# Remainder products in runs of two steps on four PSUM banks, and column sums of two rows together, in the gradient kernel of a spectral and gated-linear block

## The chip, the cores and the metric

The kernel runs on one core of one Trainium2 chip. The metric is the device time of one execution in microseconds; before the change it was 1488.78 us, the median of three runs (1486.05 to 1489.39). The kernel consists of one launch that computes the forward result and all gradients.

The engines are named as the profile names them: PE is TensorE (the matrix unit), PEld its weight loads, DVE is VectorE, ACT is ScalarE, POOL is GpSimd, SP is SyncE. Matrix results land in PSUM, which has eight banks of 512 fp32 values on each of 128 partitions.

## The reference

The reference is a block of a network with its gradients. Input x is 2048 rows of 576. Six rows of modulation come from a condition vector c. Then:

```python
h = layernorm(x) * (1 + ca) + sa
x = x + ga * irfft2(rfft2(h) * (w_r + 1j * w_i))
h = layernorm(x) * (1 + cb) + sb
g, u = h @ w_gate, h @ w_up          # 576 -> 4608
x = x + gb * ((g * u) @ w_down)      # 4608 -> 576
```

It returns this x and the gradients, for a given output gradient, of x, w_r, w_i, w_gate, w_up, w_down, c and w_mod (the matrix that makes the modulation). All tensors are bf16.

Two parts matter here. The products g and u have 576 as their contracted length: four full pieces of 128 and one of 64 for each. And the gradients of two modulation rows are sums over all 2048 rows of the gradient of h, and of that gradient times the normalized x: sums down the columns, which the kernel makes on PE with a matrix of ones.

## The kernel before

**Stages.** The kernel first turns the output gradient, computes the layer norms and the forward Fourier products, and, mixed in between as filler work for PE, the product of the output gradient with w_down transposed (`ghh_couple`, L364 to L403), which it stores in HBM. Then comes the longest part, a loop over 18 blocks of 256 hidden columns (`for p in range(NP)`, 239 to 1178 us). Then follow the backward pass of the second layer norm, the Fourier products backwards, and the last stage (from about 1365 us), a loop over 16 rows of 128 tokens that makes the gradient of x (`for j in range(18)`, L1393 on, shifted so that the pieces of three rows are under way at once). Forward output rows (`y_piece`, L1094 to L1121, matmuls at L1106) are filler for PE in the last stages.

**One block of the loop.** `gu_block(p)` computes g and u for 256 hidden columns and all 2048 tokens: two halves `fb` of 128 columns by four slices `sb` of 512 tokens, eight steps. After it, in program order: loads of the weights of the next block, the weight gradients of block p-1 (`grads`, filler turned straight on here), and the product that gives the gradient of the second layer norm's output (`gh2_block`, L963 to L977).

**A step** has ten matmuls of 512 columns: four full ones for g, four full ones for u, and one remainder of 64 rows for each. The remainder of g lies in rows 64 to 127 of the array, that of u in rows 0 to 63 (L802 and L803), and the two run side by side, into two different banks. ACT then copies g and u out of PSUM (L816, L817), and DVE makes g*u, and the products of a stored row block `ghh` with u and with g (L818 to L820). The copies go to a ring `g_r` of six buffers; the products to `xT`, which the next parts read. After the last slice of a half, g*u is stored to HBM on SP's queue (L822).

**The order now.** `gu_four` takes four steps at once. Steps 0 and 1 do their full matmuls first, then the remainders of all four steps follow in one run, then steps 2 and 3 do their full matmuls. Each of the four steps has its own pair of PSUM banks, by a fixed table, so that all eight are in use:

```python
GU_BANKS = ((0, 1), (2, 3), (6, 7), (4, 5))
```

A block so has two runs of four remainder pairs. In block 0 the order of the steps is another: (0,0) (0,1) (0,2) (1,0) and then (1,1) (1,2) (0,3) (1,3), since the last quarter of `h2T` (the turned input) arrives late.

**The last stage.** For each row j, PE does the inverse transform's last parts (`stage_bi`, L579 to L583; `stage_ai`, L593), ACT copies the gradient out as `gh`, DVE multiplies it by the normalized row `n` into `q`, and both go on to the gradient of x (L1408 to L1422). One row later, `column_sums(gq.pop(j - 2), 6, j - 2, 64)` adds the two rows to running sums in banks 6 and 7: four matmuls of 64 columns of ones (L1041), two halves by two operands. The operands of three rows are kept: `gh_r` and `q_r` are rings of three buffers.

**What sets the order.** PE's instructions stand in the order in which they are written (`tc.manual_schedule(engines={PE})`). The queues of the other engines are put in order by the planner of the tile framework, which may issue a load before work that is written ahead of it. Waits are set from the reads and writes of each buffer. `Fill` is a list of closures with an estimated cost each; `fill.run(us)` issues as many as the given time holds.

Of the kernel before, what the change touches and what calls it, by code (L numbers as in the profile page):

```python
# [14 lines left out]
MUL = mybir.AluOpType.mult  # L15
# [7 lines left out]
D = 576  # L23
F = 4608
NP = 18
# [56 lines left out]
def build(ctx, tc, A_x, A_w_r, A_w_i, B_w_gate, B_w_up, B_w_down, c_in, w_mod, grad_out,  # L82
          out_0, out_1, out_2, out_3, out_4, out_5, out_6, out_7, out_8):
    nc = tc.nc
    pe, ve, ac, po, sp = nc.tensor, nc.vector, nc.scalar, nc.gpsimd, nc.sync
# [10 lines left out]
    hh_d = dram("hh_d", [8, 128, 2 * NP, 256])  # L96
# [9 lines left out]
    bank = psp.tile([128, 8, 512], FP32, name="bank")  # L106
# [29 lines left out]
    def span(base, n, size):  # L136
        return [base + i * size for i in range(n)]

    GO, H2P = 9984, 28416
    H2T, ACC = 48896, 69376  # L140
    ST = 106240
# [16 lines left out]
    h2T = V(H2T, [16, 5, 128])  # L158
    acc = V(ACC, [16, D], FP32)

    mm, tt, ts, act = pe.matmul, ve.tensor_tensor, ve.tensor_scalar, ac.activation
# [48 lines left out]
    with tc.manual_schedule(engines={PE}):  # L210
# [485 lines left out]
        g_r = Ring(span(ST + 21504, 6, 1024), [512])  # L696
# [35 lines left out]
        def load_ghh(i):  # L732
            t = ghh_r.next()
            ghh[i] = t
            po.dma_start(t[:], ghh_d[i // 2, :, i % 2, :])  # L735
# [50 lines left out]
        def sbk():  # L786
            sbank[0] += 1
            return sring[sbank[0] % len(sring)]

        GU_BANKS = ((0, 1), (2, 3), (6, 7), (4, 5))  # L790

        def gu_four(p, steps):

            w = wgu[p]

            def cols(k):
                fb, sb = steps[k]
                return slice(128 * fb, 128 * fb + 128), slice(4 * sb, 4 * sb + 4)

            def rem(k):  # L800
                (bg, bu), (fs, js) = GU_BANKS[k], cols(k)
                mm(bank[:, bg, :], w[64:128, 8, fs], h2T[64:128, js, 4, :], k > 1, k < 2)  # L802
                mm(bank[:, bu, :], w[0:64, 8, fs], h2T[0:64, js, 3, :], k > 1, k < 2)  # L803

            def full(k):
                (bg, bu), (fs, js) = GU_BANKS[k], cols(k)
                for m in range(4):
                    mm(bank[:, bg, :], w[:, m, fs], h2T[:, js, m, :], k < 2 and m == 0, k > 1 and m == 3)  # L808
                for n, m in enumerate((0, 1, 2, 4)):
                    mm(bank[:, bu, :], w[:, 4 + n, fs], h2T[:, js, m, :], k < 2 and n == 0, k > 1 and n == 3)  # L810

            def evac(k):
                (bg, bu), (fb, sb) = GU_BANKS[k], steps[k]
                i, cs = 2 * p + fb, slice(512 * sb, 512 * sb + 512)
                g, u = g_r.next(), g_r.next()
                ac.copy(g[:], bank[:, bg, :])  # L816
                ac.copy(u[:], bank[:, bu, :])  # L817
                tt(xT[:, 0, fb, cs], g[:], u[:], MUL)  # L818
                tt(xT[:, 1, fb, cs], ghh[i][:, cs], u[:], MUL)  # L819
                tt(xT[:, 2, fb, cs], ghh[i][:, cs], g[:], MUL)  # L820
                if sb == 3:
                    sp.dma_start(hh_d[:, :, i, :].rearrange("g f x -> f g x"), xT[:, 0, fb, :].rearrange("f (g x) -> f g x", g=8))  # L822
            for k, (fb, sb) in enumerate(steps):
                i = 2 * p + fb
                if i + 2 < 2 * NP and i + 2 not in ghh and i != 1:
                    load_ghh(i + 2)
            full(0)
            full(1)
            for k in range(4):
                rem(k)  # L830
                if k < 2:
                    evac(k)
            full(2)
            evac(2)
            full(3)
            evac(3)

        def gu_block(p):

            order = [(fb, sb) for fb in range(2) for sb in range(4)]  # L840
            if p == 0:
                order = [(fb, sb) for fb in range(2) for sb in range(3)] + [(0, 3), (1, 3)]
            for k in (0, 4):
                gu_four(p, order[k:k + 4])
            if p == 0:
                load_ghh(3)

        def transposes(k):
            for fb in range(2):
# [187 lines left out]
        def column_sums(srcs, b, j, w):  # L1037

            for h in range(2):
                for i, a in enumerate(srcs):  # L1040
                    mm(bank[w * i:w * i + w, b + h, 0:288], ones[:, 0:w], a[:, 288 * h:288 * h + 288], j == 0, j == 15, skip_group_check=True)  # L1041
# [184 lines left out]
        RA, RB = ST, ST + 84480  # L1226
# [138 lines left out]
        gl_r = Ring(span(RA + 3456, 3, 1152) + [ACC + 15616], [D])  # L1365
        e_r = Ring(span(RA + 6912, 2, 1152), [288], FP32)
        H_r = Ring(span(RA + 9216, 2, 1152), [D])
        gh_r = Ring(span(RA + 11520, 2, 1152) + [ACC + 12160], [D])
        tg_r = Ring(span(RA + 13824, 2, 1152) + [RB + 3 * U], [D])
        t2_r = Ring(span(RA + 16128, 2, 1152), [D])  # L1370
        q_r = Ring(span(ST + 93312, 2, 1152) + [ACC + 13312], [D])
        wmT = V(ACC, [9, D])
        R2 = V(ACC + 10368, [D])
        o8l = V(RB + 11520, [9, D])
# [20 lines left out]
        for j in range(18):  # L1395
            if j < 16:
                if j and j + 2 < 16:
                    load_xg(j + 2)
                Hs[j] = stage_bi(j, Gt, e_r, H_r)
            if j < 2:  # L1400
                store_rev(6 + j, gws[6 + j])
            if 1 <= j < 17:
                jj = j - 1
                stage_ai(Hs[jj])
                gh = gh_r.next()
                ac.copy(halves(gh), bank[:, 2:4, 0:288])
                n = xl[jj]
                act(n[:], n[:], ACT.Identity, bias=nmr1[:, jj:jj + 1], scale=rstd1[:, jj:jj + 1])  # L1408
                gn, t2, q, s = tg_r.next(), t2_r.next(), q_r.next(), s_r.next()
                gq[jj] = [gh, q]  # L1410
                opc = mod[:, SCA, :]
                tt(gn[:], gh[:], opc, MUL)
                tt(q[:], gh[:], n[:], MUL)
                tt(t2[:], q[:], opc, MUL)
                act(gn[:], gn[:], ACT.Copy, scale=rstd1[:, jj:jj + 1], accum_out=s[:, 0:1])
                act(t2[:], t2[:], ACT.Copy, scale=nrs1[:, jj:jj + 1], accum_out=s[:, 1:2])
                ts(s[:, 0:1], s[:, 0:1], -1.0 / D, None, MUL)
                act(t2[:], n[:], ACT.Identity, bias=s[:, 0:1], scale=s[:, 1:2])
                tt(gn[:], gn[:], t2[:], ADD)
                tt(gn[:], gn[:], gl[jj][:], ADD)  # L1420
                o1 = gn
                po.dma_start(o1_v[:, jj, :], o1[:])  # L1422
                fill.run(2.2)
            fill.run(2.2)
            if j > 1:
                column_sums(gq.pop(j - 2), 6, j - 2, 64)
            while mdone < min(18, 6 * j // 5):
                k, i = mdone // 3, mdone % 3
                mod_grad(*mgs[k], i)
                if i == 2 and k + 2 < 6:  # L1430
                    load_wm2(mgs[k + 2][0], mgs[k + 2][2])
                mdone += 1
            if 5 <= j < 14:
                i = j - 5
                sp.dma_start_transpose(out=wmT[:, i, :], in_=w_mod[:, 128 * i:128 * i + 128])
# [100 lines left out]
```

## Time and profile before

| | value |
|---|---|
| profiled execution | 1488.78 us |
| its span, first to last instruction | 1486.9 us |
| PE busy | 1450.2 us (98%), 11108 matmuls |
| DVE busy | 765.9 us (52%) |
| ACT busy | 541.4 us (36%) |
| POOL busy | 347.6 us (23%) |
| granted PE clock, mean | 0.996 |
| remainders of g (L802) | 144, 379 ns each |
| column sums (L1041) | 64, 298 ns each |

The profile is of one execution. Matmuls overlap in it: each row's duration reaches from its start to its modelled end, so that matmuls which start 216 ns apart show 380 ns each. What a matmul costs on PE is therefore read from the distance of the starts. In a list of instructions in order of time, the columns are the start in us, the duration in us, engine, line, operation, operands with their shape (rows times columns of the array, then partitions by elements), and in brackets the idle time ahead of it and what ended it. In a table of stretches, the columns after the stretch's length are the busy time of PE, PEld, DVE, ACT and POOL with their instruction counts, then the granted clock, the share of the transfer engines, and GB/s.

### The profile page before, as it was taken

To read this page: it belongs to the slowest core of one execution; us is meant where nothing else is said; L and a number is where in the kernel's file an instruction comes from. 1 tells how busy PE (TensorE), PEld (TensorE's weight loads), DVE (VectorE), ACT (ScalarE), POOL (GpSimd) and SP (SyncE) were. 2 spreads that over 40 slices of the span, in tenths; PEclk is the share of its full clock that TensorE was granted. 3 is DMA by queue.
4 is the path that set the end of the run, shared out by engine and by line. 5 is a ranking of instruction groups with operands and counts; after the bars stand their busy time and mean duration, and the time that the engine had idled before them with its cause. 6 is when DMAs were issued, how large, how long until landed. Compare 5 with 4: busy or idle time off the path is not lost.

```text
span 1486.9 us, 28249 instructions
## 1 busy us (share of the span) xinstructions
PE 1450.2 (98%) x11108; PEld 973.0 (65%) x11108; DVE 765.9 (52%) x1651; ACT 541.4 (36%) x1048; POOL 347.6 (23%) x510
## 2 busy tenths in 40 slices
PE   8999999999999999999999999999999998999898
PEld 5444443677677677677677677677677666677666
DVE  6533596533533543543543543543543687678665
ACT  6756675212212212222222222222222366334566
POOL 1344322113213213213203203203202013232211
PEclk9999999999999999999999999999999999999999
DMA  9657986978568558559558558548558389667763
GB/s 346 180 148 161 228 238 163 213 144 186 126 117 188 127 113 191 123 115 193 126 110 188 118 122 196 123 110 196 126 102 182 78 238 293 218 210 199 241 222 101
DMA packets 417050, 252.79 MB, mean 170 GB/s; under 512 B 319730, under 2 KB 384692, under 8 KB 416660
## 3 DMA queue, kind: packets, MB, share of 16 engines
q1 hardware_dynamic: 388706, 166.53, 49.4%
q0 software_dynamic: 27440, 83.65, 18.3%
q8 instruction: 87, 1.43, 0.4%
q10 hardware_dynamic: 770, 0.80, 0.2%
q14 instruction: 47, 0.39, 0.1%
HBM read 98.52 MB, written 76.26 MB: 118 GB/s over the span
## 4 chain that ended last, share of the span: by engine, by line
PE 79%; DVE 6%; DMA 6%; ACT 4%; issue 3%; SPq 1%; POOL 1%; DVEq 0%; ACTq 0%; POOLq 0%
PE bank L808 9%; PE bank L857 8%; PE bank L810 8%; PE bank L904 8%; PE bank L908 8%; PE bank L963 5%; PE bank L1106 5%; PE bank L966 5%; PE bank L965 5%; PE bank L964 5%; PE bank L371 3%; PE bank L375 2%; PE bank L802 2%; DMA arena<-in_w_mod_dram 2%; PE bank L924 2%
## 5 line engine op out<-in xcount | busy, mean ns | idle before, releaser
L977 DVE TENSOR_TENSOR arena<-arena,bank 128x576 f32<-128x576 f32 x256 | 192.8, 753 | 305.1 <-PE bank L966 305.1
L816 ACT CAST arena<-bank 128x512 bf16<-128x512 f32 x144 | 86.5, 601 | 395.8 <-PE bank L803 387.5
L966 PE MATMUL bank<-arena 128*128 128x288 bf16 x576 | 164.5, 286 | 0.0
L963 PE MATMUL bank<-arena 128*128 128x288 bf16 x576 | 164.0, 285 | 0.4 <-DVE arena L975 0.2
L965 PE MATMUL bank<-arena 128*128 128x288 bf16 x576 | 164.3, 285 | 0.0
L964 PE MATMUL bank<-arena 128*128 128x288 bf16 x576 | 164.0, 285 | 0.0
L1106 PE MATMUL bank<-arena 128*128 128x288 bf16 x1152 | 151.5, 290 | 2.2 <-ACT arena L1109 2.2
L904 PE MATMUL bank<-arena 128*128 128x256 bf16 x1152 | 149.5, 273 | 1.9 <-DVE arena L890 1.8
L908 PE MATMUL bank<-arena 128*128 128x256 bf16 x1152 | 149.3, 273 | 0.0
L808 PE MATMUL bank<-arena 128*128 128x512 bf16 x576 | 148.2, 380 | 0.0
L810 PE MATMUL bank<-arena 128*128 128x512 bf16 x576 | 147.8, 379 | 0.0
L1106 PEld LDWEIGHTS <-arena 128*128 128x128 bf16 x1152 | 112.7, 99 | 35.4 <-issue 5.6
L857 PE MATMUL bank<-arena 128*128 128x288 bf16 x1024 | 128.1, 286 | 0.0
L820 DVE TENSOR_TENSOR arena<-arena 128x512 bf16<-128x512 bf16 x144 | 60.8, 422 | 123.3 <-ACT arena L816 116.1
L904 PEld LDWEIGHTS <-arena 128*128 128x128 bf16 x1152 | 110.8, 98 | 18.6 <-issue 5.2
L908 PEld LDWEIGHTS <-arena 128*128 128x128 bf16 x1152 | 112.3, 98 | 13.7
L857 PEld LDWEIGHTS <-arena 128*128 128x128 bf16 x1024 | 100.2, 98 | 28.2
L735 POOL DMA_DIRECT2D arena<-ghh_d x36 | 19.9, 553 | 393.2 <-DVE arena L819 385.8
L909 ACT CAST arena<-bank 128x256 bf16<-128x256 f32 x144 | 52.9, 373 | 144.6 <-PE bank L908 144.6
L810 PEld LDWEIGHTS <-arena 128*128 128x128 bf16 x576 | 56.4, 98 | 67.9
L808 PEld LDWEIGHTS <-arena 128*128 128x128 bf16 x576 | 53.4, 98 | 71.6 <-issue 15.3
L817 ACT CAST arena<-bank 128x512 bf16<-128x512 f32 x144 | 85.7, 595 | 12.1 <-PE bank L810 11.6
(269 smaller groups left out, 2304.8 us busy)
## 6 DMA issues: line engine op xcount, KB each, us to landing
ghh_d<-arena POOLq DMA_DIRECT2D x72, 256.0 KB, 3.9
arena<-ghh_d POOLq DMA_DIRECT2D x36, 512.0 KB, 5.8
hh_d<-arena SPq DMA_DIRECT2D x36, 512.0 KB, 4.1
arena<-hh_d SPq DMA_DIRECT2D x32, 576.0 KB, 7.1
out_dram<-arena POOLq DMA_DIRECT2D x67, 144.0 KB, 4.8
out_dram<-arena POOLq DMA_DIRECT2D x36, 256.0 KB, 5.1
arena<-in_B_w_down_dram POOLq DMA_DIRECT2D x18, 288.0 KB, 4.5
arena<-in_B_w_gate_dram POOLq DMA_DIRECT2D x18, 256.0 KB, 3.5
```

The source lines that it names most:

```text
L808: mm(bank[:, bg, :], w[:, m, fs], h2T[:, js, m, :], k < 2 and m == 0, k > 1 and m == 3)
L810: mm(bank[:, bu, :], w[:, 4 + n, fs], h2T[:, js, m, :], k < 2 and n == 0, k > 1 and n == 3)
L816: ac.copy(g[:], bank[:, bg, :])
L857: mm(bank[:, b0 + h, 0:288], sf[:, 0, fb, j, :], go[:, j, 288 * h:288 * h + 288], j == 0, j == 15)
L904: mm(bank[:, st["b"], 0:256], h2p[:, j, 128 * m:128 * m + 128], sf[:, 1 + w, :, j, :], j == 0, False)
L908: mm(bank[:, st["b"], 0:256], h2p[:, j, 128 * m:128 * m + 128], sf[:, 1 + w, :, j, :], False, j == 15)
L963: mm(o, xT[:, 1, 0, cs], wT[p][:, 0, 0, hs], True, False)
L964: mm(o, xT[:, 2, 0, cs], wT[p][:, 0, 1, hs], False, False)
L965: mm(o, xT[:, 1, 1, cs], wT[p][:, 1, 0, hs], False, False)
L966: mm(o, xT[:, 2, 1, cs], wT[p][:, 1, 1, hs], False, True)
L977: tt(dst, dst, src, ADD)
L1106: mm(bank[:, yb, 0:288], hl[:, fb % 18, 128 * (j % 2):128 * (j % 2) + 128], wdr[:, fb, 288 * h:288 * h + 288], fb == 0, fb == 35)
```

## The change

`gu_four` becomes `gu_step`, one step at a time. A step takes two banks from a ring of the four banks 0 to 3 (`sbk()`). Steps with an even `sb` do their full matmuls and then their remainder pair; steps with an odd `sb` do their remainder pair first and then the full ones. The remainders of an even step and of the odd step behind it so stand together. The load of `ghh` number 3 moves from behind block 0 to ahead of its last step.

In the last stage, the column sums are made on odd j only, for the two rows j-3 and j-2 together, and the rings of their operands get a fourth buffer each, in memory that is free there.

```diff
-        GU_BANKS = ((0, 1), (2, 3), (6, 7), (4, 5))
-
-        def gu_four(p, steps):
-
+        def gu_step(p, fb, sb):
+            i = 2 * p + fb
+            if i + 2 < 2 * NP and i + 2 not in ghh and (i != 1 or sb == 3):
+                load_ghh(i + 2)
+            js = slice(4 * sb, 4 * sb + 4)
+            cs = slice(512 * sb, 512 * sb + 512)
+            fs = slice(128 * fb, 128 * fb + 128)
+            bg, bu = sbk(), sbk()
             w = wgu[p]
...
-            full(0)
-            full(1)
-            for k in range(4):
-                rem(k)
-                if k < 2:
-                    evac(k)
-            full(2)
-            evac(2)
-            full(3)
-            evac(3)
+            odd = sb % 2
+
+            def rem():
+                mm(bank[:, bg, :], w[64:128, 8, fs], h2T[64:128, js, 4, :], odd == 1, odd == 0)
+                mm(bank[:, bu, :], w[0:64, 8, fs], h2T[0:64, js, 3, :], odd == 1, odd == 0)
+            if odd:
+                rem()
+            for m in range(4):
+                mm(bank[:, bg, :], w[:, m, fs], h2T[:, js, m, :], odd == 0 and m == 0, odd == 1 and m == 3)
+            for k, m in enumerate((0, 1, 2, 4)):
+                mm(bank[:, bu, :], w[:, 4 + k, fs], h2T[:, js, m, :], odd == 0 and k == 0, odd == 1 and k == 3)
+            if not odd:
+                rem()
+            g, u = g_r.next(), g_r.next()
+            ac.copy(g[:], bank[:, bg, :])
+            ac.copy(u[:], bank[:, bu, :])
+            tt(xT[:, 0, fb, cs], g[:], u[:], MUL)
+            tt(xT[:, 1, fb, cs], ghh[i][:, cs], u[:], MUL)
+            tt(xT[:, 2, fb, cs], ghh[i][:, cs], g[:], MUL)
+            if sb == 3:
+                sp.dma_start(hh_d[:, :, i, :].rearrange("g f x -> f g x"), xT[:, 0, fb, :].rearrange("f (g x) -> f g x", g=8))
 
         def gu_block(p):
 
             order = [(fb, sb) for fb in range(2) for sb in range(4)]
             if p == 0:
                 order = [(fb, sb) for fb in range(2) for sb in range(3)] + [(0, 3), (1, 3)]
-            for k in (0, 4):
-                gu_four(p, order[k:k + 4])
-            if p == 0:
-                load_ghh(3)
+            for fb, sb in order:
+                gu_step(p, fb, sb)
...
-        gh_r = Ring(span(RA + 11520, 2, 1152) + [ACC + 12160], [D])
+        gh_r = Ring(span(RA + 11520, 2, 1152) + [ACC + 12160, ACC + 16768], [D])
...
-        q_r = Ring(span(ST + 93312, 2, 1152) + [ACC + 13312], [D])
+        q_r = Ring(span(ST + 93312, 2, 1152) + [ACC + 13312, ACC + 17920], [D])
...
-            if j > 1:
-                column_sums(gq.pop(j - 2), 6, j - 2, 64)
+            if j > 1 and j % 2:
+                for i in (j - 3, j - 2):
+                    column_sums(gq.pop(i), 6, i, 64)
```

## The prediction

> **What bounds the kernel now.** I read the page first, then the busy time by stretches, then TensorE's timeline in three places (the gate and up products, an older stage that already has the order the change brings, the last stage), then ScalarE's timeline beside the first, and the waits of the last stage.
>
> The page says that TensorE works through the whole span at full clock:
>
> ```profile
> span 1486.9 us, 28249 instructions
> PE   8999999999999999999999999999999998999898
> PEclk9999999999999999999999999999999999999999
> ```
>
> The stretches say the same more exactly: from 465 to 1170 us, where the gate and up blocks lie, PE is busy for all 705 us; in the last stage (1350 on) it has holes.
>
> ```profile
> 465.00:1170.00 705.00, 705.00 (x5481) 502.22 (x5479) 300.01 (x554) 158.05 (x330) 145.24 (x204) 1.00 0.64 141
> 1350.00:1400.00 50.00, 47.82 (x386) 34.59 (x384) 37.09 (x87) 26.17 (x57) 11.48 (x21) 1.00 0.75 233
> 1400.00:1440.00 40.00, 37.27 (x284) 25.16 (x283) 26.99 (x79) 24.67 (x51) 9.94 (x17) 0.96 0.78 244
> ```
>
> "Busy" can hide short stops, so I checked one gate and up block by its starts. It runs from 438.76 (first full product) to 454.73 (first matmul of the next kind), 15.97 us. Its first half in TensorE's timeline (start, duration, line):
>
> ```profile
> 441.35 1.03 PE L810 MATMUL bank<-arena 128*128 128x512 bf16 x4
> 442.31 0.39 PE L802 MATMUL bank<-arena 64*128 64x512 bf16 x1
> 442.31 0.39 PE L803 MATMUL bank<-arena 64*128 64x512 bf16 x1
> ...
> 442.97 0.38 PE L802 MATMUL bank<-arena 64*128 64x512 bf16 x1
> 442.97 0.38 PE L803 MATMUL bank<-arena 64*128 64x512 bf16 x1
> 443.28 1.04 PE L808 MATMUL bank<-arena 128*128 128x512 bf16 x4
> ```
>
> Full matmuls start 0.216 us apart (28 of them from 443.28 to 449.33). The 64-row remainders go two at a time, a pair every 0.216 us. The run of them costs more at its two ends: four full ones from 441.35 are through at 442.21, the run starts at 442.31 (0.10 late); its four pairs need 0.864, but the next full matmul comes 0.97 after the first pair (0.11 late). So entering and leaving the remainders costs 0.20 us a run. The block adds up with nothing over: 64 x 0.216 + 8 pairs x 0.216 + 2 runs x 0.20 = 15.95 against 15.97. There is no stop in it that a different use of banks could take away. A whole iteration repeats every 55.6 us (the remainder runs at 442.31 and 1165.11 lie 13 iterations apart), without holes.
>
> The dO-times-Wd stage has the order that the change brings, runs of two pairs (its remainders are L378 and L379):
>
> ```profile
> 66.38 1.03 PE L375 MATMUL bank<-arena 128*128 128x512 bf16 x4
> 67.34 0.39 PE L378 MATMUL bank<-arena 64*128 64x512 bf16 x1
> 67.34 0.39 PE L379 MATMUL bank<-arena 64*128 64x512 bf16 x1
> 67.56 0.38 PE L378 MATMUL bank<-arena 64*128 64x512 bf16 x1
> 67.57 0.38 PE L379 MATMUL bank<-arena 64*128 64x512 bf16 x1
> 67.88 1.04 PE L371 MATMUL bank<-arena 128*128 128x512 bf16 x4
> ```
>
> 66.38 + 0.864 = 67.24, start at 67.34: 0.10. 67.34 to 67.88 is 0.54, less two pairs (0.432): 0.11. Again 0.20 a run, whatever its length.
>
> **The change: gate and up.** The number of matmuls, copies, products and transfers is the same; their order and banks change.
>
> Runs of remainders: before, two per block, 36 in 18 blocks. After, an even step ends with its pair and the odd step behind it begins with its own, so each couple of steps makes one run: four per block. In block 0 the order of steps is (0,0) (0,1) (0,2) (1,0) (1,1) (1,2) (0,3) (1,3), the second number giving the parity; that makes the runs [1,2] [3] [4,5] [6,7] [8], five. Blocks 1 to 17: 17 x 2 extra x 0.20 = +6.8 us. All on PE, which has no hole there to take it: on the path in full. Block 0: 3 extra, +0.6, less a shorter wait. There the pair of step (0,3) could have started at 251.02 (0.22 behind the pair at 250.80) but waited for a transfer of h2T until 251.73. In the new order that pair comes 6 x 8 x 0.216 + 6 x 0.216 + 3 x 0.20 + 0.10 = 12.37 us behind the block's start at 239.04, at 251.41, and waits 0.32 instead of 0.71: -0.4. Block 0: +0.2. Sum of the part: +7.0 us.
>
> Banks: all eight in fixed pairs become a ring of four (0 to 3), so a couple is written again two steps later. Does PE wait for ScalarE's copies? Their rows:
>
> ```profile
> 442.79 0.59 ACT L816 CAST arena<-bank 128x512 bf16<-128x512 f32 x1 [19.30 <-PE bank L803]
> 443.27 0.59 ACT L817 CAST arena<-bank 128x512 bf16<-128x512 f32 x1
> ```
>
> A copy starts 0.48 behind the start of the matmul it waits for (442.31), and two take 0.48 + 0.59 = 1.07. So a couple is free 1.55 us behind the start of its last pair. An even step's couple is written again after the odd step's pair and eight full matmuls, 0.216 + 0.216 + 0.11 + 1.73 = 2.27 us behind that start; an odd step's couple after the next even step's eight full ones and two pair places, about 2.2 us behind its last matmul. 0.6 us or more to spare: cost nothing, covered by 2.2 us of matmuls a step against 1.07 of ScalarE and three VectorE products of some 0.34 us spacing. If a copy came over 0.6 us late, that cover would be gone, at the excess per step.
>
> The Trainium skill, in "Perfetto Trace Analysis", section "Matmul Optimizations", wants all eight PSUM banks used, and so speaks against this part; by it the copies would come into view, at most 144 x 1.07 = 154 us, and the rows above say none of it. "TensorE: Matmul & The Clock Gate", section "Single matmul latency", gives a lone warm matmul about 166 ns over its streaming; were each end of a run to pay that, my estimate from that page for the 37 extra runs would be 12 us, and the measured 0.20 a run makes it 7.4.
>
> Loads: the loads of ghh stand at the same step boundaries as before; only number 3 moves by one step within block 0 (POOL's queue), and is needed in block 1, some 20 us later. The hh stores on SP and the weight loads on POOL wait for the same reads, within a few us, and are used at the next block, tens of us off. Cost nothing.
>
> **The change: column sums.** Today 16 runs of four 64-column matmuls, one a row; after, eight runs of eight. In the last stage:
>
> ```profile
> 1438.99 4.57 PE L1106 MATMUL bank<-arena 128*128 128x288 bf16 x36
> 1443.49 0.44 PE L1041 MATMUL bank<-arena 128*64 128x288 bf16 x4
> 1443.86 0.42 PE L579 MATMUL bank<-arena 128*128 128x288 bf16 x2
> ```
>
> The 36 matmuls start 0.1224 apart and are through at 1443.39; the run comes 0.10 later, and takes 0.37 where two pairs need 0.245: 0.22 us a run for entering and leaving. Eight fewer: -1.76 us of PE time. Not all is on the path: PE waits in this stage for others.
>
> ```profile
> PE bank L581 <- DVE arena L588: 2.6, 3, 1.7
> PE bank L1106 <- ACT arena L1109: 2.2, 3, 1.1
> ```
>
> Apart from one stop of 0.4 us at 1446.2 they lie before 1434, and a PE that is there 0.2 us sooner waits as much longer. The runs at 1437.54 and behind (the last eight rows, four runs saved) lie in a stretch that the chain of waits gives to PE almost throughout. So at least 4 x 0.22 = 0.9, at most 1.76; I take the middle, -1.3. The added buffer for gh and q only makes the wait for two rows possible: today a row's buffers are written again three rows later, after its sums, and no PE or ScalarE wait stands at them. The sums of row 14 move behind those of 15's place, ahead of the R2 copy; PE's work to the end is the same.
>
> **Sum.** +7.0 - 1.3 = +5.7 us on the profiled execution's 1488.78 (span 1486.9 and 1.9 around it), which is also the median of the three runs: 1494.5.
>
> **Rivals.**
> 1. The last stage gains nothing: the 0.2 us steps are all eaten by waits for VectorE. +7.0: 1495.8. The holes before 1434 speak for it, the PE chain behind against.
> 2. Other side, not slower: only PE's order is written by hand; the other queues are planned anew, and in the last stage VectorE's H product (L588) could come early enough that PE's waits for it and for the y copy go. They are worth 2.6 + 2.2 = 4.8 us: 1494.5 - 4.8 = 1489.7, no measurable change. It decides once more than some 3 us of these go. Against it: the L1109 waits hang on input transfers that the change leaves alone (the chain shows loads of A_x of 3 to 6 us there).
> 3. The same, to the bad: a queue order that adds a wait of the size of the largest now (1.7 us) once or twice in the last stage: +1.7 to +3.4, up to 1498.
> 4. Four banks are too few: copies come late by over 0.6 us in some steps. At 0.1 us a step 144 x 0.1 = 14 us: 1509. For it: in the older stage, where two couples turn, a remainder did wait 2.19 us for its copy (L383, at 235.46) while ScalarE had other rows. Against it: the slack worked out, and that ScalarE has nothing but these copies in a block.
> 5. The change does not do what it says: the extra ends are hidden and only the sums count: 1487.5. Against it stand the two 0.20s, on PE itself.
>
> **How the numbers follow.** Forecast 0.62, rival 1 0.16, rival 2 0.06, rival 3 0.10, rival 4 0.03, rival 5 0.03. A measurement tells about 0.2% (3 us) from no change: slower holds the forecast, 1, 3, 4: 0.91; same, 2 and a part of 5: 0.07; faster 0.02. Forecast and rival 1 span 1494.0 to 1495.8; the three runs before lie between 1486.05 and 1489.39, so a median may sit up to 2.7 lower by this alone, and rival 3 reaches 1498. Range 1491.0 to 1498.0; 2 and 4 and 5 are left out.
>
> **What would show it.** Right: runs of two remainder pairs every 4 us in the blocks, each 0.20 us over; a block of 16.36 us; an iteration of 56.0 instead of 55.6; the last stage's runs of eight matmuls 0.71 us long, and that stage about a microsecond shorter. Wrong: PE idle before the full products released by the ScalarE copies; an iteration still of 55.6; a last stage that moves by more than 2 us either way.

## The result and the profile after

| | before | after |
|---|---|---|
| median (range, number of runs) | 1488.26 us (1486.05 to 1489.39, 4) | 1498.84 us (1498.26 to 1499.59, 4) |
| profiled execution | 1488.78 us | 1498.26 us |
| its span | 1486.9 us | 1496.5 us |
| PE busy | 1450.2 us | 1457.6 us |

The change makes the kernel slower: after over before is 1.0073, with the interval 1.0056 to 1.0091. That is about 10.6 us, where 5.7 were forecast; 1498.84 lies outside the range of 1491 to 1498. The sign was right, the size was not.

The page of after, its span and the row of busy times:

```profile
span 1496.5 us, 28276 instructions
PE 1457.6 (97%) x11108; PEld 969.4 (65%) x11108; DVE 773.4 (52%) x1651; ACT 549.0 (37%) x1048; POOL 347.4 (23%) x510
```

The number of matmuls is the same, and PE's busy time is 7.4 us higher. To find where the span's 9.6 us arose I cut TensorE's timeline at four landmarks that both kernels have: the first full gate product, the first `gh2` product behind the last block, the first matmul of the last stage (L579), and the first matmul of the tail (before L1442, after L1424).

| us | before | after | difference |
|---|---|---|---|
| start to the first gate product | 239.04 | 238.88 | -0.16 |
| the loop over 18 blocks | 938.49 | 947.22 | +8.73 |
| between the loop and the last stage | 190.72 | 189.29 | -1.43 |
| the last stage | 109.13 | 111.49 | +2.36 |
| the tail | | | +0.1 |

The loop and the last stage are the two places that the change touches; both are worse than forecast (+7.0 and -1.3).

**The blocks look as forecast.** TensorE's timeline of after in one block (start, duration, line; L807 and L809 are the full products, L802 and L803 the remainders):

```profile
1170.57 1.03 PE L809 MATMUL bank<-arena 128*128 128x512 bf16 x4
1171.53 0.39 PE L802 MATMUL bank<-arena 64*128 64x512 bf16 x1
1171.54 0.39 PE L803 MATMUL bank<-arena 64*128 64x512 bf16 x1
1171.76 0.38 PE L802 MATMUL bank<-arena 64*128 64x512 bf16 x1
1171.76 0.38 PE L803 MATMUL bank<-arena 64*128 64x512 bf16 x1
1172.07 1.04 PE L807 MATMUL bank<-arena 128*128 128x512 bf16 x4
```

Runs of two pairs, as predicted, one every 4.1 us. Entering: 1170.57 + 4 x 0.216 = 1171.43, start at 1171.53, 0.10 late. Leaving: 0.54 from the first pair to the next full product, less two pairs of 0.216: 0.11. The block runs from 1169.71 to 1186.10, 16.39 us against 16.36 forecast and 15.97 before. No row of a block shows idle time released by the ScalarE copies.

The whole iteration, by the start of the Wd gradient in two blocks that follow each other, first in before (L857):

```profile
510.33 8.00 PE L857 MATMUL bank<-arena 128*128 128x288 bf16 x64
565.93 8.00 PE L857 MATMUL bank<-arena 128*128 128x288 bf16 x64
```

and in after:

```profile
513.72 8.00 PE L838 MATMUL bank<-arena 128*128 128x288 bf16 x64
569.75 8.00 PE L838 MATMUL bank<-arena 128*128 128x288 bf16 x64
```

56.03 us in after against 55.60 in before: +0.43 for two more runs, 0.215 a run.

**One wait stands in the loop in addition**, in block 1, where the period is 57.51 us instead of 56.03. TensorE's and ScalarE's timelines of after there (in brackets the idle time ahead and what ended it):

```profile
304.66 1.03 PE L885 MATMUL bank<-arena 128*128 128x256 bf16 x8 [1.32 <-ACT arena L911]
303.48 0.87 ACT L976 ACTIVATE arena<-arena 128x576 bf16<-128x576 bf16 x1 [14.54 <-DMA arena<-x_d]
304.25 0.35 ACT L911 CAST arena<-bank 128x256 bf16<-128x256 f32 x1
```

ScalarE stood 14.5 us before a transfer of x_d with the activation of `keep_n`, and the copy that PE needed stood behind it.

**The last stage is longer, not shorter.** PE's waits in it, after (waiting line and line waited for; us in total, number, longest):

```profile
PE bank L581 <- DVE arena L588: 3.5, 2, 2.4
PE bank L1087 <- ACT arena L1090: 3.2, 2, 2.5
PE bank L593 <- ACT arena L1387: 1.1, 1, 1.1
```

The first two are waits that before had too, larger now: 6.7 us against 4.8. The third, for the copy of `gh`, is new.

**Part of it is no property of the kernel.** After, TensorE's timeline behind the first of the waits for L1090:

```profile
1391.22 1.27 PE L1087 MATMUL bank<-arena 128*128 128x288 bf16 x9
1394.96 5.14 PE L1087 MATMUL bank<-arena 128*128 128x288 bf16 x27 [2.48 <-ACT arena L1090]
1400.03 0.68 PE L1022 MATMUL bank<-arena 128*64 128x288 bf16 x8
```

The 27 matmuls took 5.14 us, where 26 distances of 0.1224 and the last one's 0.29 make 3.47. The busy time by stretches of after shows why, ahead of the two waits of over 2 us and around them (the granted clock is the third number from the end):

```profile
1375.00:1393.00 18.00, 17.37 (x138) 12.56 (x137) 12.40 (x35) 7.02 (x14) 5.84 (x10) 1.00 0.65 202
1393.00:1402.00 9.00, 7.04 (x46) 4.52 (x46) 4.31 (x12) 7.47 (x18) 1.10 (x2) 0.81 0.79 253
1430.00:1442.00 12.00, 9.56 (x69) 6.03 (x67) 10.54 (x33) 8.55 (x19) 4.29 (x7) 0.86 0.60 167
```

The granted clock falls behind the wait. Such a slow spell costs 1.7 us each time (9.00 x (1 - 0.81), 12.00 x (1 - 0.86)). Before has one in its last stage, after two, and after run again (after_again, below) none. So a single profile's stage is compared both as it is and less its spells: before 109.1 and 107.4, after 111.5 and 108.1.

### The profile page after: what moved, and what is told of

Its sections match the earlier page's. It is cut to its first block, busy times and chain, and to the rows that moved or that the text cites. A ratio compares the mean times of both kernels' runs of the same rounds, so it can differ in the third digit from the quotient of the medians.

```text
span 1496.5 us, 28276 instructions
## 1 busy us (share of the span) xinstructions
PE 1457.6 (97%) x11108; PEld 969.4 (65%) x11108; DVE 773.4 (52%) x1651; ACT 549.0 (37%) x1048; POOL 347.4 (23%) x510
## 3 DMA queue, kind: packets, MB, share of 16 engines
q8 instruction: 87, 1.43, 0.4%
## 4 chain that ended last, share of the span: by engine, by line
PE 80%; DVE 8%; DMA 5%; ACT 4%; issue 2%; SPq 0%; POOL 0%; DVEq 0%; ACTq 0%; POOLq 0%
PE bank L807 9%; PE bank L809 8%; PE bank L838 8%; PE bank L885 8%; PE bank L889 8%; PE bank L944 5%; PE bank L947 4%; PE bank L945 4%; PE bank L946 4%; PE bank L1087 4%; PE bank L371 3%; PE bank L375 3%; PE bank L802 3%; DMA arena<-in_w_mod_dram 2%; PE bank L905 2%
## 5 line engine op out<-in xcount | busy, mean ns | idle before, releaser
L813 ACT CAST arena<-bank 128x512 bf16<-128x512 f32 x144 | 84.3, 585 | 384.8 <-PE bank L803 376.9
L807 PE MATMUL bank<-arena 128*128 128x512 bf16 x576 | 148.6, 380 | 0.0
L809 PE MATMUL bank<-arena 128*128 128x512 bf16 x576 | 147.8, 379 | 0.0
L807 PEld LDWEIGHTS <-arena 128*128 128x128 bf16 x576 | 50.4, 98 | 78.1 <-issue 30.6
L809 PEld LDWEIGHTS <-arena 128*128 128x128 bf16 x576 | 56.4, 98 | 67.9
L814 ACT CAST arena<-bank 128x512 bf16<-128x512 f32 x144 | 84.8, 589 | 22.5 <-PE bank L809 22.5
```

The costliest lines, as they stand in the source:

```text
L807: mm(bank[:, bg, :], w[:, m, fs], h2T[:, js, m, :], odd == 0 and m == 0, odd == 1 and m == 3)
L809: mm(bank[:, bu, :], w[:, 4 + k, fs], h2T[:, js, m, :], odd == 0 and k == 0, odd == 1 and k == 3)
```

## The experiments

Ratios are to the kernel before on the same chip, with a 95% interval. "Last stage" and "period" are measured as above.

### The two parts alone: g_only, g_only_c, g_only_d, s_only, s_only_c

g_only is before with the new `gu_step` alone, that is after with the last stage as before:

```diff
-        gh_r = Ring(span(RA + 11520, 2, 1152) + [ACC + 12160, ACC + 16768], [D])
+        gh_r = Ring(span(RA + 11520, 2, 1152) + [ACC + 12160], [D])
...
-        q_r = Ring(span(ST + 93312, 2, 1152) + [ACC + 13312, ACC + 17920], [D])
+        q_r = Ring(span(ST + 93312, 2, 1152) + [ACC + 13312], [D])
...
-            if j > 1 and j % 2:
-                for i in (j - 3, j - 2):
-                    column_sums(gq.pop(i), 6, i, 64)
+            if j > 1:
+                column_sums(gq.pop(j - 2), 6, j - 2, 64)
```

> The gate and up part of the change alone; the column sums stay one row at a time with three buffers. Theory 1 (the price is the ends of the remainder runs, 0.20 to 0.215 us each, and the last stage's loss belongs to the sums): blocks 2 to 16 repeat every 56.03 us instead of 55.60, the last stage from its first L579 to the first row sum of R2 keeps its 109.1 us, and the total is 7 to 9 us above the kernel before, the upper end if the 1.3 us wait of the first weight gradient products for a ScalarE copy in block 1 comes again. Theory 2 (the gate and up part shifts the last stage against its transfers): the last stage takes 111 us or more here, total 9 to 11 us above. Theory 3 (four banks too few): PE shows waits for the copies L813 or L814 in the blocks.

s_only is the opposite: these hunks alone, on before.

> The column sums of two rows together with the fourth buffer, on the kernel before; gate and up products as before. The prediction's working: 0.9 to 1.76 us faster, last stage 107.4 to 108.2 us against 109.1. Theory 1 (the pairing moves PE work behind waits, and the queues of ScalarE, VectorE and SyncE come out in another order): last stage 111 to 112 us, total 2 to 3 us slower, with a PE wait for the copy of the output row of over 2 us near the first sums. Theory 2 (the loss belongs to the shift by the gate and up part): last stage 108, total about 1 us faster.

The same two kernels again, beside after, on other chips:

> The gate and up part alone, again, on one chip with the change and the sums alone. Ratio 1.005 to 1.006 (7.5 to 9 us), with a loop of 946.2 us.

> The column sums alone, again. Leaving out 6.5 us of sums saved 2.1 us, a third; the pairing takes 1.76 us of PE time away, so by that price -0.6 us, ratio 0.9985 to 1.001. If the pairing's new queue order costs what the change shows over the gate and up part: ratio 1.0015 or more.

> The gate and up part alone, third time. The loop gives 7.7 us, 1.0052. Two runs gave 1.0051 and 1.0061, with chances of a further 1 us behind the loop. If that further 1 us is real, 1.0058 or more again; if not, 1.0055 or less.

| | median, us | ratio | period, us | last stage, us |
|---|---|---|---|---|
| g_only | 1497.14 | 1.0051 (1.0034 to 1.0069) | 56.03 | 110.01 |
| g_only_c | 1497.61 | 1.0061 (1.0045 to 1.0076) | 56.03 | 110.15 |
| g_only_d | 1497.78 | 1.0050 (1.0032 to 1.0068) | 56.03 | 109.05 |
| s_only | 1488.66 | 0.9999 (0.9986 to 1.0011) | 55.61 | 109.14 |
| s_only_c | 1491.66 | 1.0014 (1.0002 to 1.0026) | 55.60 | 109.54 |

The gate and up part costs some 8 us (the mean of the three ratios is 1.0054). Its loop is 945.96 to 946.86 us long against 938.49: +7.7, the median of the three being 946.16. The column sums, forecast at -1.3, change nothing in one measurement and cost 2 us in the other.

### The buffers alone don't matter: s_3buf

The paired sums with the two rings left at three buffers.

```diff
-            if j > 1:
-                column_sums(gq.pop(j - 2), 6, j - 2, 64)
+            if j > 1 and j % 2:
+                for i in (j - 3, j - 2):
+                    column_sums(gq.pop(i), 6, i, 64)
```

> The column sums of two rows together, with the rings of gh and q left at three buffers, on the kernel before. The queues stand in the same order as with four. If the fourth buffer is needed for the pairing to go without a wait: slower than the run with four buffers by 1 us or more, with ScalarE's copy of gh or VectorE's q waiting for PE's sums. If it is not: the same within 1 us.

1489.55 us, 1.0011 (0.9999 to 1.0024), last stage 108.82 us. The instructions of every engine stand in the same order as in s_only; the fourth buffers change no queue, and by this the time no more than can be measured.

### Four banks or eight: g_8banks

The order of after in the blocks, but with the fixed pairs of before, turned through all eight banks. To show it on top of after (the last stage as before):

```diff
+        gstep = [-1]
+
...
-            bg, bu = sbk(), sbk()
+            gstep[0] += 1
+            bg, bu = ((0, 1), (2, 3), (6, 7), (4, 5))[gstep[0] % 4]
```

> The gate and up part alone as in the first run, but each step takes the next of the four fixed pairs over all eight banks, as the kernel before has them. Order of the matmuls as after. Theory 1 (runs of remainders are the whole price): iteration 56.03 us, the same as with four banks. Theory 3 (four banks cost): 55.6 to 55.9 us.

1495.62 us in the profiled execution; loop 946.02 us. Its Wd gradients in TensorE's timeline:

```profile
512.36 8.00 PE L841 MATMUL bank<-arena 128*128 128x288 bf16 x64
568.39 8.00 PE L841 MATMUL bank<-arena 128*128 128x288 bf16 x64
```

The period is 56.03 us, the same to the hundredth as with four banks. The banks cost nothing, as forecast. The Trainium skill's wish for all eight banks ("Perfetto Trace Analysis", section "Matmul Optimizations") makes no difference here, 56.03 against 56.03.

### The price of a run: g_8runs

Every step ends with its own pair: eight runs a block instead of four (the last stage as before).

```diff
-            odd = sb % 2
+            odd = 0
```

> The gate and up part with every step ending in its own remainder pair, no step starting with it: eight runs a block in place of four (36 before, 73 in the change, 144 here). Theory 1 (0.20 to 0.215 us for each run): 71 runs more than the change's, blocks repeat every 56.03 + 4 x 0.21 = 56.9 us, 14 to 15.5 us slower than the gate and up part alone. Rival (a run costs less when it is short, as two pairs against four would hint): under 56.6 us.

1510.58 us. Its Wd gradients in TensorE's timeline:

```profile
518.76 8.01 PE L838 MATMUL bank<-arena 128*128 128x288 bf16 x64
575.65 8.01 PE L838 MATMUL bank<-arena 128*128 128x288 bf16 x64
```

The period is 56.89 us. With 36, 73 and 144 runs of remainders in the program the loop is 938.49, 946.15 and 961.84 us long. By period, two more runs a block cost 0.43, four more 0.86: 0.215 us a run both times (by the whole loop, block 0 included, 0.207 and 0.221). This line through three points is the explanation of the gate and up part; within some 0.01 us a run it leaves nothing for banks or copies. "TensorEngine Tiling (Array Packing)", section "Key Properties", in the Trainium skill says that a change of the tiling mode drains the TensorE, without a price; what these runs show is 0.215 us for going to 64-row tiles and back.

### The wait in block 1: after_again, after_k

after_again is the unchanged kernel after once more. after_k is after with `keep_n` of row 0 moved from block 1 to block 2:

```diff
-                    if i == 7:
-                        keep_n(p)
+                    if i == 7 and p > 1:
+                        keep_n(p if p > 2 else 1)
+                    if i == 15 and p == 2:
+                        keep_n(2)
```

> The changed kernel itself, timed again on one chip with the runs below. If its two parts simply add (gate and up alone measured 1.0051 of the kernel before, column sums alone 0.9999), the ratio is 1.005 to 1.006, 7 to 9 us, and the 1.3 us wait of block 1 and the 111.5 us of the last stage that its first profile shows were that execution's. If the parts act on one another, the ratio stays at 1.007 or more, and its profile shows a last stage over 111 us again.

> The changed kernel with the saving of normalized row 0 (load of x1, ScalarE's normalizing, store) moved from block 1 to block 2, so that in block 1 ScalarE has no load to wait for ahead of the copies of the weight gradients. If the wait of 1.3 us in block 1 stands in most executions: 1 to 1.5 us faster than the change. If it was that one execution's: the same within 0.7 us.

after_again: 1498.37 us, 1.0083 (1.0070 to 1.0096); its loop is 946.15 us, and the wait in block 1 isn't there. after_k: 1498.79 us, 1.0069 (1.0052 to 1.0087), the same as after beside it (below). So the 1.48 us of block 1 belong to that one profiled execution: of the ten profiles that have the new order in the blocks and `keep_n` in its old place, one has a wait of over 1 us there. It was a tempting cause and explains nothing of the median.

### Is PE's time in the last stage on the path: no_sums

Column sums of rows 0 and 15 alone, before's other lines.

```diff
-            if j > 1:
+            if j in (2, 17):
                 column_sums(gq.pop(j - 2), 6, j - 2, 64)
```

> The kernel before with the column sums left out for rows 1 to 14 (the sums are then over rows 0 and 15 alone); 56 matmuls and 14 runs of 64-column matmuls fewer, some 14 x 0.47 = 6.5 us of PE time. Prediction's step (PE bounds the second half of the last stage): at least 8 x 0.47 = 3.8 us faster, last stage 105 us or less against 109.1. Theory 1 (the last stage is set by the chain of transfers, ScalarE and VectorE, and PE's time there is spare): less than 1.5 us faster, last stage 108 us or more, PE's waits up from 5 to 10 us or more.

1485.04 us, 0.9986 (0.9975 to 0.9996). Fourteen runs of 0.37 + 0.10 us, 6.6 us of PE's time, are gone, and by the medians 2.1 us come out: a third. The last stage is 105.49 us, 3.6 shorter. PE's waits in it, no_sums:

```profile
PE bank L581 <- DVE arena L588: 5.1, 4, 1.8
PE bank L1106 <- ACT arena L1109: 2.0, 3, 1.0
PE bank L579 <- ACT arena L585: 0.4, 1, 0.4
```

Waits for the H product (L588) grow from 2.6 us in three places to 5.1 in four: what PE saves, it partly waits. This kernel's queues are planned anew too, so the third is no pure measure.

### More buffers: x5_row

If input transfers hold the last stage up, a fifth buffer for x should help.

```diff
-        x_r = Ring(span(RA, 3, 1152) + [ACC + 14464], [D])
+        x_r = Ring(span(RA, 3, 1152) + [ACC + 14464, ACC + 33600], [D])
```

> The kernel before with a fifth buffer for the rows of x in the last stage, so that a row's load waits less for the buffer to be given back. Theory 1 (the chain row of x loaded, ScalarE's normalizing, the copies queued behind it, is what PE waits for): ScalarE's waits for loads of A_x fall from 29.6 us, PE's waits in the last stage fall from 5.2 to under 2.5 us, 2 to 4 us faster. Rival (the order of VectorE and ScalarE's own work sets the pace): within 1 us of the kernel before.

1491.49 us, 1.0031 (1.0020 to 1.0042): slower, with a resource added and no work. ScalarE's waits for loads of x in the last stage did not shrink (21.1 us, before 21.2), PE's waits there grew from 4.8 to 7.0 us. The planner had put the queues of the other engines in another order. That this order is the cause is not shown, as no run has the fifth buffer in the old order; it turned the question from buffers to orders.

### The order of the other queues: pair_oldq, row_newq, after_oldq

PE's order in this program is written by hand; the tile framework plans the others. By the traces, the shortest edit from before's order to that of s_only moves 4 instructions on ACT, 39 on DVE, 4 transfers on SP and one on POOL, all in the last stage; the gate and up part alone moves one transfer, on POOL, in block 0. Two kernels separate the sums from the order. pair_oldq has the paired sums, but the last stage's instructions of the four engines are held in the order that before has, by ordering edges between neighbours that set no semaphore. row_newq has single-row sums (with the fourth buffers in place), and the engines are held in the order that was planned for the pairs. In the traces the last stage's instructions stand in the orders intended. The core of both (`_ORDER` lists the source lines of the last stage in the order wanted, engine by engine):

```diff
-        fill.flush()
+        fill.flush(); _enforce(tc, LOG)
...
+def _enforce(tc, log):
+    for e, want in _ORDER.items():
...
+        seq = [next(it[key]) for key in want]
+        for a, b in zip(seq, seq[1:]):
+            tc.add_manual_dep(b, a.name, mybir.DependencyInfo(mybir.DependencyClass.NoSync, mybir.DependencyReason.DATA), reason="order")
```

> The column sums of two rows together (four buffers) on the kernel before, but with the instructions of ScalarE, VectorE, GpSimd and SyncE in the last stage held in the order that the kernel before has. Only PE's order differs from before. If the planner's new queue order is what ate the pairing's gain: 0.6 to 1.8 us faster than the kernel before, ratio 0.9988 to 0.9996, and 1 to 3 us faster than the sums alone with their own queue order (0 to 2.3 us above before). If the moved PE work itself costs (less work ahead of a wait, more behind it): no faster than before, 0 to 2 us slower.

> The converse: column sums a row at a time, as before, with the queues of the other engines in the last stage held in the order that the planner gives the paired sums. If the queue order costs: 1 to 3 us slower than before, ratio 1.0007 to 1.002. If the moved PE work costs: within 0.7 us of before.

| | sums by row | sums in pairs |
|---|---|---|
| order of before | before 1487.44; stage 109.13 | pair_oldq 1486.94, 0.9993 (0.9981 to 1.0004); stage 107.62 |
| order planned for pairs | row_newq 1489.28, 1.0017 (1.0006 to 1.0028); stage 111.34 | s_only 0.9999 and 1.0014; stage 109.14 and 109.54 |

The stages by TensorE's timeline, each time the stage's first row and the first one behind it, before:

```profile
1368.25 0.41 PE L579 MATMUL bank<-arena 128*128 128x288 bf16 x2
1477.38 0.36 PE L1442 MATMUL bank<-arena 1*128 1x1 bf16 x5
```

pair_oldq:

```profile
1367.33 0.41 PE L579 MATMUL bank<-arena 128*128 128x288 bf16 x2
1474.95 0.36 PE L1443 MATMUL bank<-arena 1*128 1x1 bf16 x5
```

and row_newq:

```profile
1367.32 0.41 PE L579 MATMUL bank<-arena 128*128 128x288 bf16 x2
1478.66 0.36 PE L1442 MATMUL bank<-arena 1*128 1x1 bf16 x5
```

In the old order the stage with pairs is 1.5 us shorter: the forecast's -1.3 and a little more. The new order, with nothing else changed, lengthens it by 2.2, and by its median the kernel by 1.8. The two cancel in s_only. This 2 x 2 is the core of the finding on the last stage; the order's effect stands on the interval of row_newq, which lies above 1, and the pairs' gain on single profiles alone: 0.9993 is no measured gain, and the six profiles with the old order and sums by row differ among themselves by 2.0 us (108.1 to 110.2).

Less the slow spells, and with all profiles taken that belong to a cell, the stages are:

| us, less slow spells | sums by row | sums in pairs |
|---|---|---|
| order of before | 108.1 (mean of six: before, the three of g_only, g_8banks, g_8runs; 107.3 to 110.1) | 106.7 (pair_oldq 105.9, after_oldq 107.5) |
| order planned for pairs | 109.6 (row_newq) | 108.7 (mean of eight: the two of s_only, s_3buf, the five of after and after_k; 107.1 to 109.9) |

The picture is the same, a little smaller: the pairs gain 0.9 to 1.4, the order costs 1.5 to 2.0. Both are less than the 2.8 us by which the profiles within one cell differ, so the sizes are rough.

Where the order acts can be seen in PE's waits. row_newq's:

```profile
PE bank L1106 <- ACT arena L1109: 2.7, 2, 1.8
PE bank L593 <- ACT arena L1406: 1.8, 1, 1.8
PE bank L581 <- DVE arena L588: 1.7, 3, 1.0
PE bank L579 <- ACT arena L585: 1.3, 1, 1.3
```

and pair_oldq's:

```profile
PE bank L581 <- DVE arena L588: 2.7, 2, 2.0
PE bank L1106 <- ACT arena L1109: 2.6, 2, 2.1
```

In sum PE waits 4.8 us in this stage in before, 5.3 in pair_oldq, 7.5 in row_newq and 8.5 in s_only. The wait of L593 for the copy of `gh` (L1406) is new, and so is that of L579 for the copy of e (L585). ScalarE's timeline of before at the place, in one row of the stage:

```profile
1434.77 0.38 ACT L585 COPY arena<-bank 128x288 f32<-128x288 f32 x1
1435.04 0.64 ACT L1406 CAST arena<-bank 128x576 bf16<-128x576 f32 x1
1438.75 0.87 ACT L1408 ACTIVATE arena<-arena 128x576 bf16<-128x576 bf16 x1 [3.07 <-DMA arena<-in_A_x_dram]
```

and of row_newq, with PE's row that waits:

```profile
1433.80 0.38 ACT L585 COPY arena<-bank 128x288 f32<-128x288 f32 x1
1438.27 0.87 ACT L1408 ACTIVATE arena<-arena 128x576 bf16<-128x576 bf16 x1 [4.09 <-DMA arena<-in_A_x_dram]
1439.04 0.62 ACT L1406 CAST arena<-bank 128x576 bf16<-128x576 f32 x1
1439.71 0.41 PE L593 MATMUL bank<-arena 128*128 128x288 bf16 x2 [1.77 <-ACT arena L1406]
```

The normalising of `n` (L1408) waits for a load of x. In the old order the copy of `gh` stands ahead of it and is done while ScalarE would wait anyway; in the new one, in this one row, it stands behind, and PE waits 1.77 us for a copy whose data had long been there. This wait is in all nine profiles of kernels with the new order (0.56 to 2.79 us) and in none of the eight with the old one (before, the three of g_only, g_8banks, g_8runs, pair_oldq, after_oldq).

after_oldq is the kernel after with the last stage's queues held in before's order by the same helper; after_c and after_d are after itself, beside the others.

> The changed kernel a third time, on one chip with its two parts alone. The loop of blocks takes 946.2 us in every profile of the new order but one, against 938.5, so 7.7 us of the 10.6 to 12 measured are accounted for; 3 to 4 are not. If they belong to the two parts together, this run stands 2.5 us or more above the gate and up part alone; if they are the spread of the stages behind the loop, within 2 us of it.

> The changed kernel, on one chip with the run above and the gate and up part alone: 1.007 of the kernel before, as before (three times 1.0069 to 1.0083).

> The changed kernel, both parts, with the queues of ScalarE, VectorE, GpSimd and SyncE in the last stage held in the order of the kernel before. If the terms add: loop +7.7, pairing -0.5 to -1.5, no new queue order, so 1.0045 to 1.005, and 2 to 3.5 us under the change on the same chip. If the change's excess over the loop has another cause: within 1 us of the change.

| | median, us | ratio | last stage, us |
|---|---|---|---|
| after_c | 1498.90 | 1.0069 (1.0053 to 1.0086) | 110.92 |
| after_d | 1498.08 | 1.0050 (1.0031 to 1.0069) | 111.62 |
| after_oldq | 1496.10 | 1.0048 (1.0033 to 1.0063) | 109.21 |

On one chip after_oldq is 2.0 us faster than after_d by the medians, 0.9 by the means, and the stage 2.4 us shorter (one slow spell in each). The ratios, which differ by 0.0002 with intervals of 0.0015 to 0.0019 to either side, don't settle it: the direction agrees with row_newq, no more. No kernel here beats the one before by more than its interval.

## Why the prediction was wrong, step by step

**Gate and up, runs of remainders (+7.0): right in mechanism, a little small.** Blocks of 16.39 us against 16.36 forecast, an iteration of 56.03 against 56.0. A run costs 0.215 us instead of the 0.20 read off two runs in the timeline; 17 x 2 x 0.215 = 7.3, and block 0, forecast at +0.2, holds the rest of the +7.7 that the loops show. The mis-size is 0.7 us.

**Banks and copies (nothing): right.** The same period with four and eight banks, and the same price a run at 73 and 144 runs. Rival 4 is out, and so is rival 5.

**Loads and stores of the blocks (nothing): right for the median.** The wait in block 1 behind `keep_n` came in one of ten profiles.

**Column sums (-1.3): this is the step that failed.** The prediction took "the middle" between 0.9 and 1.76 us saved, and said of the rest that the buffers' only effect was to make the wait for two rows possible and that "PE's work to the end is the same". The price of a run was right on PE: in after a run of eight starts 0.10 us late (1472.97 + 36 x 0.1224 = 1477.38, start at 1477.48) and takes 0.61, the 0.71 that was forecast. When all else stands still the stage is 1.5 us shorter in the one profile of pair_oldq, though the kernel's time shows no clear gain (0.9993). But all else does not stand still. Pairing the sums in PE's hand-written order made the planner move 4 instructions on ACT, 39 on DVE and 4 transfers on SP, and this order costs 1.5 to 2.2 us of the stage (row_newq, +1.8 us by its median). On the mean of the profiles of each kind the stage with pairs in the new order is 110.2 us, that with the old sums and order 109.3; less the slow spells 108.7 and 108.1. So it gains nothing and loses 0.5 to 0.9, where -1.3 stood: a miss of about 2 us. The prediction's own sign of being wrong, a last stage that moves by more than 2 us, came in the first profile (+2.36), with a slow spell of 1.7 in it.

**Rival 3 had the mechanism and its price.** It named a queue order that adds a wait of 1.7 us once or twice, up to 1498, and was given 0.10. Rival 2, the same cause to the good, got 0.06. Both sides of an unknown order were thus seen, and then left out of the sum as if the likeliest order were the old one; the profile held nothing that spoke for that.

**Not in the prediction at all: slow spells.** It priced waits at their length. Between the loop and the end of the last stage the profiles hold from none (after_again) to five portions (s_only_c) of 1.7 us, and much of the spread between executions of one kernel goes with them: after_again's profiled one, with none, was its fastest at 1493.53 us against a median of 1498.37. They blur every profile by some microseconds; the profiles' mean numbers give no sign that after has more of them (1.6 in its five profiles with after_k, 2.2 in the five of the gate and up part alone, 2 in before's one).

**What stays open.** +7.7 for the loop and +0.5 to +0.9 for the last stage make 8.2 to 8.6 us; the four measurements of after itself (1.0073, 1.0083, 1.0069, 1.0050) mean 1.0069, 10.2 us. The two parts alone give 8.0 and about 1. Some 1.6 to 2 us have no place in these profiles. Between the loop and the last stage, where the change has nothing, the profiles run from 187.77 to 192.83 us, less their slow spells from 186.0 to 189.0, and those of after (187.6 to 188.9) are no longer than before's (189.0); the remainder was not to be found there. Where after was timed beside the gate and up part alone, it is only 1.3 us (after_c) and 0.3 us (after_d) slower by the medians. The mean clock listed with every execution offers a place for about half of the remainder, not shown: the time lost to a lowered clock, span times one less the clock, is 7.2 us on average in 96 executions of before and 8.2 in the 25 of after and after_k, a difference known to some 0.6 us.

## What to carry to other kernels

Where TensorE has no holes, count how often a kind of tile is entered and left, not only how many matmuls there are: here 0.215 us a time, read off the starts of three neighbouring groups and confirmed to within 0.02 us by the period of a block. Where a framework plans the queues, an edit of one engine's order is an edit of all of them: compare the instruction orders before the edit is priced, and hold the old order to see what the edit itself is worth. In such an order look for an instruction that waits for a load and has moved ahead of a copy that TensorE needs.

## What the hardware showed that was not expected

**Slow spells come in portions on a fixed grid of 3.413 us, and not behind every wait.** I cut all nineteen profiles into slices of 2 us from 1180 us to the end of the last stage, and marked those with a granted clock under 0.99. They hold 39 spells; one costs 1.70 to 1.72 us each time (the sum of the slices' lengths times one less their clock), as 3.4 us at half clock would, and three are double, 3.40 to 3.42. Against that I set PE's waits of 0.9 us or more in the same stretch, and counted those with a spell beginning from 2.5 us ahead of their end to 3.5 us behind it:

| length of the wait, us | waits | with a spell |
|---|---|---|
| 0.9 to 1.3 | 32 | 2 (both just behind a longer wait) |
| 1.3 to 1.7 | 25 | 5 |
| 1.7 to 2.2 | 45 | 12 |
| 2.2 to 3 | 14 | 7 |
| over 3 | 12 | 10 |

The longer the wait, the likelier the spell, but one of the same length may bring it or not. The trace's records of the granted clock show more. In each of the profiles all of these spells begin whole multiples of 3.413 us apart (to within 0.001 of that time), and hold half the clock for 3.413 us or twice that. So there is a fixed grid, and what tells is the idle time that falls into one window of it. I took the 6846 windows of all profiles from 245 us to the end of the last stage that have the full clock themselves. Of the 23 with PE idle for 1.94 us or more, every one was followed by a spell; of the 57 with 1.46 to 1.94 us, 16 were; of the 6766 with less, none.

A count of work separates them better still: each matmul counted at 0.216 us for 512 columns, from 50 ns behind the start of its row on, times the share of the 128 x 128 array that it uses (a 64-column sum counts half). Of the 40 windows in which this fills less than 0.375 of the time, 39 were followed by a spell, and of the others none. The 50 ns and the 0.375 were fitted to these same spells, so this describes them and has not been tested on others. After's wait of 2.48 us for L1090 (1392.48 to 1394.96) lies in one window, and the next, from 1395.80 on, is slow. A window's edge can also cut a wait in two. s_only, TensorE's timeline behind a wait longer than those of after:

```profile
1438.76 0.41 PE L593 MATMUL bank<-arena 128*128 128x288 bf16 x2 [2.79 <-ACT arena L1406]
1439.01 4.57 PE L1106 MATMUL bank<-arena 128*128 128x288 bf16 x36
```

36 matmuls in 4.57 us, full rate: the grid has an edge at 1437.51, which divides the wait into 1.54 and 1.25 us. The prediction priced each wait at its length; a wait of 2.2 to 3 us cost 1.7 us more in half of the cases. The Trainium skill, "TensorE: Matmul & The Clock Gate", section "HAM oscillation — how this bites in real kernels", warns of idle gaps over about 3.4 us; here many a shorter one was enough. The same page, section "What's actually happening", says that the full clock comes back after a busy window of about 3.4 us, which fits the portions of 3.4 us at half clock. No run varied the gap by itself.

**An added buffer made the kernel slower by 0.31%** (x5_row, interval 0.20 to 0.42%); the new queue order that came with it is the likely cause, not shown.
